# Scores by token halves, paired gate and value weights, and a new issue order in a fused attention and gated MLP kernel

## The chip, the core and the metric

The kernel runs on one core of a Trainium2 chip. A core has five engines with an instruction queue each: TensorE (matrix products, "PE" in the profile, its weight loads "PEld"), VectorE ("DVE"), ScalarE ("ACT"), GpSimd ("POOL") and SyncE ("SP", which here only issues transfers). TensorE writes to PSUM, and VectorE and ScalarE carry results from there into SBUF. The metric is the device time of one execution in microseconds (us), as the median of several runs. A profiled execution gives a trace in which every instruction has a start, a duration and what it waited for.

## The reference

```python
# attention: x is (8, 8, 512, 64), state is (8, 8, 32, 64)
scores  = x @ state^T / sqrt(D);     a  = softmax over the 32 state rows
xread   = a @ state
scores2 = state @ x^T / sqrt(D);     a2 = softmax over the 512 tokens
sread   = a2 @ x
y = concat([xread, sread], axis=2)   # 8 batches, 8 heads, 512 + 32 rows, 64
# gated MLP on y as (8 * 544, 512)
gate = sigmoid(y @ w_gate);  val = y @ w_val      # d_ff = 1536
out  = (gate * val) @ w_out
```

Inputs and output are float32; the kernel computes its products in bfloat16.

## The kernel before

**Algebra.** For the 512 token rows of a batch the product `xread @ w` is never formed from `xread`. The kernel multiplies the state of all heads with the gate and value weights first (`SW`, 8 heads of 32 rows by 1536 columns for each of the two weights), and then multiplies the softmax probabilities with `SW`. So one batch needs: scores, exponentials, sums and products for the probabilities `ab`; their transposes `aT`; `SW`; 12 groups `gv_mm` (four matmuls with 512 columns: two for the gate, two for the value); tanh of the gate half (`gv_th`, ScalarE); the product `glu` (`gv_glu`, VectorE); and 12 groups `out_mm` (four matmuls with `w_out`). The 32 state rows of each batch are read by `rd_mm` and `rd_fin` into `xr`, gathered in `XS`, and go through the MLP together at the end, as "batch 8".

**Tiles.** Tokens are taken as `(p c)`: 128 partitions times four chunks `c`. Head `h` is `2 * j + e` with four pairs `j`. `xT` holds x transposed, in `[j, c]` blocks of 128 by 128; `E1` holds the exponentials in float32 and `Eb` the same in bfloat16. The scores of one batch are 16 matmuls with 64 columns, each with a block of `xT` as its weights; they come in two halves `i` of two head pairs each (`S_mm(b, i, ...)`, `S_exp(b, i)`, `n_sum`, `n_mul`), so each half needs all four chunks of its two pairs.

**Two ways to transpose.** For batches 0 and 1 x and `ab` are transposed on TensorE (`xT_mm`, `aT_mm`) and copied out of PSUM. From batch 2 on, SyncE issues transposing transfers, four for x (`at_xT_dma`, one for each chunk, line 140) and four for `ab` (`aT_dma`, line 211), and one for `xr` (`rd_dma`).

**SW.** `sw_visit(b, lo, n, ...)` computes some columns of `SW` for one batch, `sw_wide(b, v)` half of all columns in three places of PSUM. Each set is eight small matmuls of 64 rows by 32 columns of weights, which lie side by side in the array. Visits of 256 columns do the gate and the value weights one after the other (`sw_mm` twice). `sw_cp` copies one PSUM tile into `SW`, on ScalarE (`act`) or VectorE (`vec`).

**Token sums.** For batches 0 to 2, `rd_mm` gets the sums of `a2` from matmuls with a column of ones, 32 for a batch, each for one head and chunk. From batch 3 on the ones stand beside the x values.

**Weights and loads.** `load_w(w, lo, n)` loads and converts columns of the gate (`w` 0) or value weights (1) through GpSimd's queue, `load_wo` a third of `w_out`, `load_sb` the states of two batches, `load_xh` x of batch 1. SyncE loads x of batch 0 in four pieces of two heads (`load_xp`); batches 2 and 3 come through GpSimd's queue, later ones through SyncE's.

**Order.** The schedule is manual: every engine executes its instructions in the order in which the program text issues them. Lines 415 to 662 are a long list for batches 0 and 1 and the start of batch 2, in which the work of several steps is interleaved by hand. `warm` issues matmuls whose results nobody uses. The loop from line 664 on then has one turn for each batch `b` from 2 to 8, with 12 steps `f`: a `gv_mm` of batch `b` and an `out_mm` of batch `b - 1` in each step, and between them the preparation of batch `nb = b + 1`: `sw_wide` at steps 0 and 6, scores at 1 and 2, sums at 2 and 3, the two products at 4 and 6, `rd_mm` at 6, the four `aT_dma` transposes after step 6, then (for batch 3 as `nb`) the cast and the transposes of the x of the next batch. PSUM has eight places: two for `GV`, one each for `OU` and `AT`, four for `SWP`.

Of the kernel before, what the change touches and what calls it, by code (L numbers as in the profile page):

```python
# [16 lines left out]
def kernel(  # L17
# [42 lines left out]
    wg = wp.tile((128, 4, dff), BF, name="wg")  # L60
    wv = wp.tile((128, 4, dff), BF, name="wv")
# [62 lines left out]
    held = {}  # L124
# [17 lines left out]
    def S_mm(b, i, place, jjs=(0, 1)):  # L142
        if jjs[0] == 0:
            held["S", b, i] = place[0].tile((128, 4, 2, 2, Ns), FP, name="Sp", tag=place[1])
        ps = held["S", b, i]
        for jj in jjs:
            j = 2 * i + jj
            for c in range(4):
                if b < 2:
                    e, c2 = c // 2, c % 2 * 2  # L150
                    nc.tensor.matmul(ps[:, c2:c2 + 2, e, jj], xTs[b][:, j, c], sTd[:, b, 2 * j + e], start=True, stop=True)  # L151
                else:
                    nc.tensor.matmul(ps[:, c, :, jj], xTs[b][:, j, c], sTz[:, b, j], start=True, stop=True)  # L153

    def S_exp(b, i):
        if b not in E1s:
            E1s[b] = ap_.tile((128, 4, 2, 4, Ns), FP, name="E1")
        nc.scalar.activation(E1s[b][:, :, :, 2 * i:2 * i + 2].rearrange("p c e j n -> p (c e) j n"),  # L158
                             held["S", b, i].rearrange("p c e j n -> p (c e) j n"), AF.Exp, scale=scale)

    def at_Eb(b):
        Ebs[b] = ap_.tile((128, 4, 2, 4, Ns), BF, name="Eb")
# [3 lines left out]
    def halfE(b, i):  # L166
        return E1s[b][:, :, :, 2 * i:2 * i + 2].rearrange("p c e j n -> p (c e) j n")

    def n_sum(b, i):
        rs = ap_.tile((128, 8, 2), FP, name="rs")  # L170
        nc.vector.tensor_reduce(rs, halfE(b, i), AX.X, ALU.add)  # L171
        ri = held["ri", b, i] = ap_.tile((128, 8, 2), FP, name="ri")
        nc.vector.reciprocal(ri, rs)

    def n_sums(b):
        rs = ap_.tile((128, 32), FP, name="rs2")
        nc.vector.tensor_reduce(rs, E1s[b].rearrange("p c e j n -> p (c e j) n"), AX.X, ALU.add)
# [3 lines left out]
    def n_muls(b, eng):  # L181
        abs_[b] = ap_.tile((128, 4, 2, 128), BF, name="ab")
        (nc.gpsimd if eng is pool else nc.vector).tensor_tensor(abs_[b].rearrange("p c e (j n) -> p (c e j) n", n=Ns), E1s[b].rearrange("p c e j n -> p (c e j) n"),
                          held["ri", b].unsqueeze(2).to_broadcast((128, 32, Ns)), ALU.mult)

    def n_mul(b, i, eng, lo=0, n=4):
        if b not in abs_:
            abs_[b] = ap_.tile((128, 4, 2, 128), BF, name="ab")
        ri, ce = held["ri", b, i], slice(2 * lo, 2 * lo + 2 * n)
        (nc.gpsimd if eng is pool else nc.vector).tensor_tensor(abs_[b].rearrange("p c e (j n) -> p (c e) j n", n=Ns)[:, ce, 2 * i:2 * i + 2],  # L190
# [559 lines left out]
```

## Time and profile before

| | |
|---|---|
| median of 3 runs | 225.36 us (224.76 to 225.91) |
| the profiled execution | 226.11 us |
| its span in the trace | 224.3 us |
| moved by DMA | 27.13 MB, mean 121 GB/s |
| TensorE's granted clock | 1.00 in every stretch |

The span runs from the first to the last event of the trace; 1.8 us of the profiled execution lie around it. "Busy" is the time in which an engine executes. In a line of the groups or of the timeline, `out<-in` names the tiles written and read, `128*128` or `64*32` behind a matmul is the part of the array that its weights fill, `x8` is the number of instructions, and the bracket at the end names the idle time before and what ended it. For TensorE the durations overlap, since matmuls are pipelined and their ends are modelled; the distance between two starts is what a matmul costs.

### The profile page before, as it was taken

To read this page: it belongs to the slowest core of one execution; us is meant where nothing else is said; L and a number is where in the kernel's file an instruction comes from. 1 tells how busy PE (TensorE), PEld (TensorE's weight loads), DVE (VectorE), ACT (ScalarE), POOL (GpSimd) and SP (SyncE) were. 2 spreads that over 40 slices of the span, in tenths; PEclk is the share of its full clock that TensorE was granted. 3 is DMA by queue.
4 is the path that set the end of the run, shared out by engine and by line. 5 is a ranking of instruction groups with operands and counts; after the bars stand their busy time and mean duration, and the time that the engine had idled before them with its cause. 6 is when DMAs were issued, how large, how long until landed. Compare 5 with 4: busy or idle time off the path is not lost.

```text
span 224.3 us, 5054 instructions
## 1 busy us (share of the span) xinstructions
PE 216.3 (96%) x2001; PEld 106.6 (48%) x2001; DVE 117.3 (52%) x204; ACT 128.6 (57%) x241; POOL 56.3 (25%) x92
## 2 busy tenths in 40 slices
PE   8788999999899999999999999999999999999994
PEld 2554444444344444444444444444444444466744
DVE  2597886476558443843583538544755334422311
ACT  4577785485566566748565666566756444423311
POOL 8299053361323027000720072003200000000001
PEclk9999999999999999999999999999999999999999
DMA  6999999842697233994653203521122111121113
GB/s 192 198 206 190 270 215 173 185 138 44 123 268 265 46 76 88 271 177 123 193 133 92 92 21 73 152 67 47 47 73 76 47 51 47 64 75 50 47 28 114
DMA packets 41911, 27.13 MB, mean 121 GB/s; under 512 B 24000, under 2 KB 38080, under 8 KB 41888
## 3 DMA queue, kind: packets, MB, share of 16 engines
q1 hardware_dynamic: 32544, 18.95, 32.8%
q0 software_dynamic: 9056, 7.67, 19.8%
q8 instruction: 15, 0.25, 0.5%
q10 hardware_dynamic: 288, 0.20, 0.3%
q14 instruction: 8, 0.07, 0.1%
HBM read 18.35 MB, written 8.91 MB: 122 GB/s over the span
## 4 chain that ended last, share of the span: by engine, by line
PE 84%; SPq 6%; DMA 5%; ACT 1%; issue 1%; DVE 1%
PE outp L333 34%; PE gvp L302 34%; PE swp L250 5%; PE gvp L305 5%; SPq L140 4%; DMA xT<-xb 2%; DMA xf<-in_x_dram 2%; SPq L211 2%; PE Sp L153 1%; PE outp L355 1%; PE rdp L225 1%; PE Sp L151 1%; SPq L83 1%; PE warm L369 1%; PE aTp L197 1%
## 5 line engine op out<-in xcount | busy, mean ns | idle before, releaser
L317 DVE SCALAR_TENSOR_TENSOR glu<-th,gvp 128x512 bf16<-128x512 f32 (+1 forms) x108 | 70.5, 658 | 83.9 <-ACT th L312 70.3
L333 PE MATMUL outp<-wo,glu 128*128 128x512 bf16 x396 | 98.2, 379 | 0.0
L302 PE MATMUL gvp<-aT,SW 128*128 128x512 bf16 x384 | 96.3, 379 | 0.1
L312 ACT ACTIVATE th<-gvp 128x512 f32<-128x512 f32 (+1 forms) x108 | 61.8, 576 | 57.5 <-PE gvp L302 44.5
L333 PEld LDWEIGHTS <-glu 128*128 128x128 bf16 x396 | 37.7, 98 | 42.2 <-issue 0.6
L302 PEld LDWEIGHTS <-SW 128*128 128x128 bf16 x384 | 36.2, 98 | 45.0 <-issue 2.8
L288 ACT CAST SW<-swp 128x512 bf16<-128x512 f32 x73 | 40.6, 586 | 7.6 <-PE swp L250 6.9
L337 ACT ACTIVATE res<-outp 128x512 f32<-128x512 f32 x33 | 19.7, 597 | 17.3 <-PE outp L333 17.3
L104 POOL COPY pre<-th 128x1 f32<-128x1 f32 x5 | 0.9, 188 | 69.6 <-ACT th L312 69.6
L116 POOL CAST xb<-xf 128x1024 bf16<-128x1024 f32 x12 | 12.3, 1042 | 15.9 <-DMA xf<-in_x_dram 15.9
L288 DVE CAST SW<-swp 128x512 bf16<-128x512 f32 x23 | 15.4, 684 | 1.3 <-PE swp L250 1.3
L346 POOL DMA_DIRECT2D out_dram<-res x2 | 1.0, 528 | 59.7 <-ACT res L337 59.7
L164 POOL CAST Eb<-E 128x256 bf16<-128x256 f32 x32 | 12.5, 433 | 10.5 <-ACT E L158 10.4
L158 ACT ACTIVATE E<-Sp 128x512 f32<-128x512 f32 x16 | 9.5, 601 | 3.9 <-PE Sp L151 2.4
L214 POOL CAST xs<-xf 128x1024 bf16<-128x1024 f32 x10 | 10.2, 1045 | 0.0
L250 PE MATMUL swp<-wg,sTc 64*32 64x512 bf16 (+1 forms) x192 | 8.7, 327 | 0.0
L190 DVE TENSOR_TENSOR ab<-E,ri 128x512 bf16<-128x512 f32 x11 | 8.5, 771 | 0.0
L171 DVE TENSOR_REDUCE rs<-E 128x16 f32<-128x512 f32 x12 | 8.1, 676 | 0.7 <-ACT E L158 0.7
L369 PE MATMUL warm<-wm 128*128 128x512 bf16 x17 | 6.6, 523 | 1.0 <-DVE wm L417 1.0
L250 PE MATMUL swp<-wv,sTc 64*32 64x512 bf16 (+1 forms) x192 | 7.5, 323 | 0.0
L250 PEld LDWEIGHTS <-sTc 64*32 64x32 bf16 x384 | 4.9, 91 | 5.4 <-issue 3.2
L305 PE MATMUL gvp<-XS,wv 128*128 128x256 bf16 x48 | 7.2, 273 | 0.0
(68 smaller groups left out, 109.3 us busy)
## 6 DMA issues: line engine op xcount, KB each, us to landing
out_dram<-res SPq DMA_DIRECT2D x24, 256.0 KB, 2.6
xf<-in_x_dram SPq DMA_DIRECT2D x4, 1024.0 KB, 7.2
xf<-in_x_dram POOLq DMA_DIRECT2D x2, 1024.0 KB, 8.1
out_dram<-res SPq DMA_DIRECT2D x15, 128.0 KB, 1.9
wo<-in_moe_w_out_dram POOLq DMA_DIRECT2D x3, 512.0 KB, 11.4
xf<-in_x_dram SPq DMA_DIRECT2D x4, 256.0 KB, 3.8
wg<-in_moe_w_gate_dram POOLq DMA_DIRECT2D x2, 512.0 KB, 8.6
wv<-in_moe_w_val_dram POOLq DMA_DIRECT2D x2, 512.0 KB, 10.9
```

The source lines that it names most:

```text
L116: cp(xbs[b].rearrange("p c h d -> p h c d")[:, lo:lo + n], (xhs if b in xhs else xfs)[b][:, lo:lo + n])
L158: nc.scalar.activation(E1s[b][:, :, :, 2 * i:2 * i + 2].rearrange("p c e j n -> p (c e) j n"), held["S", b, i].rearrange("p c e j n -> p ( ...
L164: nc.gpsimd.tensor_copy(Ebs[b][:, c], E1s[b][:, c])
L214: pool(xs.rearrange("p c h d -> p h c d")[:, lo:lo + n, :, :D], xfs[b][:, lo:lo + n])
L250: nc.tensor.matmul(pss[e][j * Ns:(j + 1) * Ns, o:o + n], sTc[rows, b, j] if b > 1 else sTd[rows, b, 2 * j + e, e], (wg, wv)[w][rows, j, lo ...
L288: cp(*sw_left.pop((b, lo, w, e)))
L302: nc.tensor.matmul(ps, SWs[b][:, g, w, fs], aTs[b][:, :, g], start=(g == 0), stop=(g == 1))
L305: nc.tensor.matmul(ps, (wg, wv)[w][:, j, fs], XS[:, :, j], start=(j == 0), stop=(j == 3))
L312: nc.scalar.activation(th, held["gv", b, f][0], AF.Tanh, scale=0.5)
L317: nc.vector.scalar_tensor_tensor(glus[b][:, f], held["th", b, f], 1.0, held["gv", b, f][1], ALU.add, ALU.mult)
L333: nc.tensor.matmul(ops[b, c], glus[b][:, f, c * 128:(c + 1) * 128], wo[:, f], start=(f == 0), stop=(f == NF - 1))
L337: nc.scalar.activation(res, ops[b, c], AF.Copy, scale=0.5)
```

## The change

Six parts. (1) From batch 2 on, a half of the scores is two chunks of tokens with all four head pairs, not two head pairs with all chunks; `E1`, `Eb`, sums and products follow (`half`, `grp`), and `aT_dma(b, i)` sends two of the four transposes. In the loop the first two go out at step 5 and the other two at step 6. (2) Gate and value weights lie in one tile `wgv`. (3) `sw_pair` computes 256 gate and 256 value columns with one matmul of 512 columns, in place of two `sw_mm`. (4) The token sums of batches 0 to 2 take all four head pairs in one matmul, 8 for a batch. (5) The hand-written list is new throughout: loads, casts, copies, the places in PSUM and the order of the groups. The matmul groups in it are the same, and so is the number of `warm` matmuls, 17. (6) Some work moves to other engines in that list: the second part of batch 2's x is still cast on GpSimd but the first on VectorE, half of batch 3's on ScalarE.

The helpers:

```diff
-    wg = wp.tile((128, 4, dff), BF, name="wg")
-    wv = wp.tile((128, 4, dff), BF, name="wv")
+    wgv = wp.tile((128, 4, 2, dff), BF, name="wgv")
+    wg, wv = wgv[:, :, 0], wgv[:, :, 1]
...
     def S_mm(b, i, place, jjs=(0, 1)):
+        if b > 1:
+            ps = held["S", b, i] = place[0].tile((128, 2, 2, 4, Ns), FP, name="Sp", tag=place[1])
+            for c in range(2):
+                for j in range(4):
+                    nc.tensor.matmul(ps[:, c, :, j], xTs[b][:, j, 2 * i + c], sTz[:, b, j], start=True, stop=True)
+            return
...
+    def half(b, i, t):
+        if b > 1:
+            return t[b][:, 2 * i:2 * i + 2].rearrange("p c e (j n) -> p (c e j) n", n=Ns)
+        return t[b].rearrange("p c e (j n) -> p (c e) j n", n=Ns)[:, :, 2 * i:2 * i + 2]
...
-    def aT_dma(b):
-        for c in range(4):
+    def aT_dma(b, i):
+        for c in range(2 * i, 2 * i + 2):
             nc.sync.dma_start_transpose(aT_tile(b)[:, c], abs_[b][:, c].rearrange("p e k -> p (e k)"))
...
-            if b < 3:
-                for c in range(4):
-                    for j in range(4):
-                        nc.tensor.matmul(rd[j * Ns:(j + 1) * Ns, e, D:], Ebs[b][:, c, e, j], ones, start=(c == 0), stop=(c == 3))
+        for e in range(2 if b < 3 else 0):
+            for c in range(4):
+                nc.tensor.matmul(rd[:, e, D:], Ebs[b][:, c, e], ones, start=(c == 0), stop=(c == 3))
...
+    def sw_pair(pss, b, lo, n):
+        for j in range(4):
+            for e in range(2):
+                rows = slice(e * 64, (e + 1) * 64)
+                nc.tensor.matmul(pss[e][j * Ns:(j + 1) * Ns].rearrange("p (w n) -> p w n", w=2),
+                                 sTc[rows, b, j] if b > 1 else sTd[rows, b, 2 * j + e, e],
+                                 wgv[rows, j, :, lo:lo + n], start=True, stop=True)
...
-            for w in range(2):
-                sw_mm(pss, b, w, lo, n, w * n)
+            sw_pair(pss, b, lo, n)
...
-                for w in range(2):
-                    sw_mm(pss, b, w, lo + 512, 256, 256 * w)
+                sw_pair(pss, b, lo + 512, 256)
```

The loop:

```diff
+                if f in (5, 6):
+                    aT_dma(nb, f - 5)
                 if f == 6:
-                    aT_dma(nb)
                     rd_dma(nb)
```

The start of the new list, which takes the place of lines 415 to 473 and on:

```python
load_xp(0, nc.sync, 6, 2)
nc.vector.memset(wm, 0.0)
warm(1, GV)
warm(2, GV)
warm(4, SWP)
zero(sTz, pool)
load_xp(0, nc.sync, 0, 2)
load_s(0, nc.scalar)
zero(sTd, vec)
make_identity(nc, ident)
load_xh(1, 0, 4)
load_xh(1, 4, 4)
cast_xp(0, vec, 0, 2)
cast_s(0, act)
warm(1, GV)
sT_mm(0, SWP)
cast_xp(0, act, 6, 2)
sT_pad(0, act)
xT_mm(0, 3, OU)
load_xp(0, nc.sync, 4, 2)
sT_pad(1, vec)
load_w(1, 256, 256)
cast_xp(0, pool, 4, 2)
xT_mm(0, 0, GV)
xT_cp(0, 0, act)
xT_mm(0, 2, SWP)
warm(1, SWP)
xT_cp(0, 3, vec)
load_w(0, 256, 256)
xT_cp(0, 2, vec)
S_mm(0, 1, GV, (0,))
load_xp(0, nc.sync, 2, 2)
S_mm(0, 0, SWP, (0,))
cast_xp(0, act, 2, 2)
xT_mm(0, 1, OU)
zero(sbz, vec)
xT_cp(0, 1, vec)
S_mm(0, 1, SWP, (1,))
...
S_exp(0, 1)
n_sum(0, 1)
...
load_w(0, 1024, 512)
...
S_exp(0, 0)
...
n_sum(0, 0)
n_mul(0, 0, vec)
load_w(1, 1024, 512)
```

Its later places that matter below: the groups of batches 0 and 1 up to the cast of batch 2 on VectorE, and the way from batch 2's scores to the loop.

```python
sw_visit(0, 1024, 512, 1)
sw_cp(0, 1024, 1, 1, vec)
aT_cp(1, None, vec)
sw_cp(0, 1024, 1, 0, act)
sw_visit(1, 1024, 512, 1)
gv_mm(0, 11, GV)
...
load_x(2, nc.gpsimd)
...
sw_cp(0, 0, 2, 0, vec)
cast_x(2, vec, 0, 4)
gv_mm(1, 4, SWP)
gv_th(0, 4)
...
gv_glu(0, 4)
...
cast_x(2, pool, 4, 4)
gv_th(1, 5)
at_xT_dma(2)
...
S_mm(2, 0, GV)
...
S_exp(2, 0)
S_mm(2, 1, OU)
S_exp(2, 1)
n_sum(2, 0)
n_sum(2, 1)
...
n_mul(2, 0, vec)
out_mm(0, 6, GV)
load_x(3, nc.gpsimd)
at_Eb(2)
n_mul(2, 1, pool)
sw_wide(2, 1)
sw_cp(2, 1, 1, 0, act)
aT_dma(2, 0)
...
aT_dma(2, 1)
...
cast_x(3, pool, 4, 4)
cast_x(3, act, 0, 4)
out_mm(0, 7, GV)
sw_wide(2, 0)
at_xT_dma(3)
```

More of the change, by code (lines that the diff above doesn't have):

```diff
@@ L522 @@
[L522 to L532 removed]
+    gv_mm(0, 11, GV)
+    sw_cp(1, 1024, 1, 0, act)
+    gv_th(0, 11)
+    gv_mm(0, 8, SWP)
+    gv_glu(0, 11)
+    gv_mm(0, 10, GV)
+    gv_th(0, 8)
+    gv_th(0, 10)
+    sw_cp(1, 1024, 1, 1, vec)
+    load_w(1, 0, 256)
+    gv_glu(0, 8)
+    sT_mm(2, AT)
+    sw_visit(1, 512, 512, 1)
@@ L664 @@
+    sw_cp(2, 0, 1, 1, vec)
     for b in range(2, B + 1):
```

449 lines of the change are left out of this document (205 added, 244 removed).

## The prediction

> **What bounds the kernel now.** I read the shares of the engines first, then the chain that ended last, then the span by stages.
>
> ```profile
> span 224.3 us, 5054 instructions
> PE 216.3 (96%) x2001; PEld 106.6 (48%) x2001; DVE 117.3 (52%) x204; ACT 128.6 (57%) x241; POOL 56.3 (25%) x92
> ```
>
> ```profile
> PE 84%; SPq 6%; DMA 5%; ACT 1%; issue 1%; DVE 1%
> ```
>
> TensorE (PE) is busy 96% and is 84% of the chain; the rest of the chain is mostly SyncE's queue (SPq) and transfers. In the stages below, the columns are the stretch, its length and each engine's busy time, then clock, DMA share and GB/s. I cut them where the matmuls of batch 0 begin to follow without a break (20.91), and at the first gate matmul of batches 2, 3, 4 and 5.
>
> ```profile
> 0.00:20.91 20.91, 17.08 (x306) 9.15 (x306) 12.59 (x26) 12.23 (x22) 15.70 (x31) 1.00 1.17 198
> 20.91:57.10 36.19, 36.19 (x408) 16.50 (x401) 26.19 (x44) 24.75 (x47) 13.61 (x17) 1.00 0.90 169
> 57.10:81.50 24.40, 23.49 (x216) 10.86 (x208) 13.33 (x23) 15.16 (x29) 5.60 (x9) 1.00 0.63 164
> 81.50:105.34 23.84, 23.50 (x216) 10.83 (x208) 12.73 (x23) 15.13 (x29) 5.57 (x9) 1.00 0.67 148
> 105.34:128.67 23.33, 23.33 (x216) 10.83 (x209) 12.73 (x23) 14.99 (x29) 5.57 (x9) 1.00 0.48 135
> ```
>
> From 20.91 on TensorE has no gaps except in the turns of batches 2 and 3. They last 24.40 and 23.84 us, the next one 23.33, with 216 matmuls in each: 1.07 + 0.51 = 1.58 us are waiting, and its cause stands in TensorE's waits (total, times, longest).
>
> ```profile
> PE Sp L153 <- DMA xT<-xb: 1.3, 2, 0.9
> ...
> PE swp L250 <- issue: 0.8, 1, 0.8
> ```
>
> So there are three places where time can go: the start before 20.91, the solid stretch 20.91 to 57.10, which only fewer or cheaper matmuls or a new stall can alter, and the 1.58 us. After 105.34 only cheaper matmuls could gain.
>
> **Matmuls that become fewer.** The changed program issues 1802 matmuls instead of 2001: 128 fewer in the gate and value weights (256 of 256 columns become 128 of 512), 72 fewer for token sums. What these cost now (start, length, instruction group; I use the distance from start to start, because the ends are modelled):
>
> ```profile
> 80.95 0.40 PE L250 MATMUL swp<-wv,sTc 64*32 64x512 bf16 x8
> 81.17 0.29 PE L250 MATMUL swp<-wg,sTc 64*32 64x256 bf16 x8
> 81.28 0.29 PE L250 MATMUL swp<-wv,sTc 64*32 64x256 bf16 x8
> 81.50 1.04 PE L302 MATMUL gvp<-aT,SW 128*128 128x512 bf16 x4
> ```
>
> Eight matmuls of 512 columns take 0.22 us, eight of 256 take 0.11. The time goes by columns and not by instructions: a pair of 0.11 + 0.11 becomes one of 0.22. I cost the edit at nothing, and the steady turn stays 23.33.
>
> ```profile
> 52.82 0.25 PE L232 MATMUL rdp<-ones,Eb 128*32 128x1 bf16 x16
> 52.92 0.33 PE L228 MATMUL rdp<-xb,Eb 128*32 128x64 bf16 x16
> 53.06 0.30 PE L232 MATMUL rdp<-ones,Eb 128*32 128x1 bf16 x16
> 53.28 0.30 PE L250 MATMUL swp<-wg,sTd 64*32 64x256 bf16 x8
> ```
>
> ```profile
> 87.44 0.40 PE L153 MATMUL Sp<-sTz,xT 128*128 128x64 bf16 x8
> 87.68 1.03 PE L333 MATMUL outp<-wo,glu 128*128 128x512 bf16 x4
> 88.54 0.81 PE L302 MATMUL gvp<-aT,SW 128*128 128x512 bf16 x3
> ```
>
> The 32 token sums of a batch take 0.10 + 0.22 = 0.32 us, four at a time side by side with 32 columns of weights. Eight take their place, each with all 128 columns of weights; the nearest row is the score matmul of that form, 0.24 us for eight. That is a gain of 0.08 for each of three batches at best and, if the wider loads hide worse, a loss of about as much: nothing, within 0.3 us in all. A big matmul costs (88.54 - 87.68) / 4 = 0.215 us.
>
> The same group of eight lasts 0.11 us where its own form follows (81.17 to 81.28) and 0.22 where another does (81.28 to 81.50). A rule of the Trainium skill speaks of this and against the edit: TensorEngine Tiling (Array Packing), Key Properties, says that a change of tiling mode drains TensorE. The trace agrees, with 0.11 us. By the rule the wide sums add one such change where weight matmuls follow them, in batch 1: the sum below would be 0.1 higher.
>
> **The start.** The new order loads heads 6, 0, 4, 2 of batch 0 (before 4, 2, 6, 0) and puts casts and copies on other engines.
>
> ```profile
> 9.54 1.26 ACT L158 ACTIVATE E<-Sp 128x512 f32<-128x512 f32 x2 [1.55 <-PE Sp L151]
> ```
>
> ```profile
> 7.48 0.43 DVE L91 CAST xf<-xf 128x512 bf16<-128x512 f32 x1 [1.16 <-DMA xf<-in_x_dram]
> ...
> 20.86 0.68 DVE L288 CAST SW<-swp 128x512 bf16<-128x512 f32 x1
> ```
>
> The last load of batch 0 lands at 7.48 and 2.06 us later the first exponential starts. After the change only its cast (0.43 by the row; ScalarE does it), four transposes and four score matmuls stand between, without the copies of the other heads that stood there: I estimate 8.7, 0.8 earlier. VectorE's sums then start at 9.35 instead of 10.17, where the first stretch below begins. From there VectorE is the narrow place: the last copy that the first group of eight after the start needs (20.86) ended at 21.54.
>
> ```profile
> 10.17:21.54 11.37, 9.65 (x18) 1.00 1.37 199
> 21.54:30.50 8.96, 8.08 (x16) 1.00 1.27 252
> ```
>
> ```profile
> L190 DVE TENSOR_TENSOR ab<-E,ri 128x512 bf16<-128x512 f32 x11 | 8.5, 771 | 0.0
> ```
>
> The first two lines are VectorE's busy times in two stretches. In the first it had 9.65 busy and 1.72 idle. The change swaps one copy for another of 0.68 and brings one product from GpSimd (0.77 by the third line), so 10.4 us. From 9.35 the copy ends at 19.8 with no idle left and at 21.5 with all of it; TensorE begins 0.63 before that, as now (21.54 - 20.91): 19.1 to 20.9.
>
> The second condition is a load. The value weights of columns 1024 on were issued at 6.03:
>
> ```profile
> 6.03 0.79 POOL L100 DMA_DIRECT2D wv<-in_moe_w_val_dram  x1
> ...
> 20.53 0.93 POOL L78 DMA_DIRECT2D xf<-in_x_dram  x1
> ...
> 30.50 1.04 POOL L116 CAST xb<-xf 128x1024 bf16<-128x1024 f32 x1 [7.55 <-DMA xf<-in_x_dram]
> ```
>
> ```profile
> DMA to landing us min/median/max: 5.9/7.9/13.0
> ```
>
> ```profile
> L111 POOL MEMSET sTz<- 128x2048 bf16 x1 | 1.8, 1822 | 0.0
> ```
>
> The landing line is for all eight weight loads, so they landed by 19.0 at the latest. In the new order GpSimd first clears a tile twice as large as now (1.82 us, so 0.9 more) and casts two heads between the issues (about 0.5, half of the cast at 30.50): with a short wait for these heads I put the issue at 7.6. The DMA share is 1.17 over the whole start, the engines are full, and the same bytes stand ahead of this load, so its landing should move less than its issue: 19.0 to 20.6. Its matmuls and a copy (0.22 and 0.68 us, less the 0.63 lead) put TensorE's start some 0.5 later with the hand-overs, 19.5 to 21.1. I take 20.2 from both, **0.7 us gained**. Whether the 0.8 us of "issue" comes back I cannot see; I count it neither way.
>
> **The solid stretch.** It holds the same 34 groups of four big matmuls, the same copies and transposes, so it keeps its 36.19 us unless a new wait comes in.
>
> ```profile
> L91 DVE CAST xf<-xf 128x512 bf16<-128x512 f32 x3 | 1.6, 538 | 4.5 <-DMA xf<-in_x_dram 4.5
> ```
>
> The change adds three waits. ScalarE casts half of batch 3, whose load is issued about when it was and well ahead; behind the cast stand copies of weight products out of PSUM, for which TensorE's next weight matmuls wait. SyncE's first half of the probability transposes waits for the first product only; behind it stand the second half, the x transposes of batch 3 and output stores. VectorE casts half of batch 2 (before GpSimd). In 21.54 to 30.50 VectorE is busy 8.08 of 8.96; two casts of 0.54 by the row above, or a little more, make 9.2 to 9.4, over by 0.2 to 0.4. Behind the cast stand the products (glu) of the gates; three pairs of PSUM buffers cover some of it. I take **0.3 us lost**, bounds 0 and 0.9.
>
> **Scores by token halves.** The first half of the scores now needs two of the four x transposes, and two of the four probability transposes leave one step earlier.
>
> ```profile
> 53.98 5.84 SPq L140 DMA_TRANSPOSE xT<-xb  x4
> ```
>
> ```profile
> 58.55 3.12 DMA xT<-xb
> ```
>
> Batch 3's four go out from 53.98 to 59.82, the last is issued at 58.55 and lands at 61.67, and the longest wait of the scores for it is the 0.9 above: they wanted it at 60.8. Two of them would have landed at about 53.98 + 1.46 + 3.12 = 58.6. The second half, two big groups (1.72 us) later, can wait until 62.5. Batch 4's queue starts earlier as well, for half of batch 3's probabilities no longer stand in it after the turn's middle. I take 1.4 of the 1.58 us, **1.4 gained**, bounds 0.5 and 1.58. Batches 5 to 7 show no such wait, and gain nothing.
>
> **Sum.** -0.7 + 0.3 + 0 - 1.4 = -1.8. The profiled execution took 226.11, so 224.3. That execution lies 0.75 above the median of 225.36; on the level of the medians it is **223.6 us**.
>
> **Rivals.**
> 1. *The loads bind the start.* DMA share 1.17 to 1.37 says that the start is full, and a new order cannot bring all weights earlier. Then TensorE starts at 20.9 as now and with 0.3 lost only 1.1 remains: 225.0, or 224.3 on the medians' level. The Trainium skill (DMA: Bandwidth & Descriptors, Issuing engines are not separate DMA queues) says that transfers of all issuers share 16 engines; this case's share above 1 agrees.
> 2. *The halves do nothing.* If the x transposes of batch 3 go out as late as now plus a stall, or the halves wait for all four landings, the 1.58 us stay: 226.11 - 0.4 = 225.7, 225.0 on that level. Against it: the landings are waited for one by one.
> 3. *VectorE waits for batch 2's x: slower.* That load was issued at 20.53 and GpSimd's cast found it landed at 30.50, 10.0 us later; only GpSimd waited for it. In the new order TensorE, from 20.2, does nine big groups (7.7), six weight visits (1.3) and three small ones of state transposes (0.24 each, as scores) before the groups that stand behind VectorE's cast: it is at 30.0. Three groups (2.6) and the first half of a fourth (0.4) go on without VectorE, to 33.0; the cast (1.1) and one product (0.7) must be done by then, so a landing until 31.2 is free. Later, each us costs one, and from 33.3 the gains of 2.1 are gone. The issue moves to 19.1 to 20.9 (five issues behind batch 1's casts, or the landing above), so 29 to 31 is likely; with the longest weight latency, 13.0, it is 33.9. At 36 the time is 226.11 - 2.1 + 4.8 = 228.8, 228.1 on that level.
>
> **Chances.** Forecast 0.53; a better start (19.2, and no loss after it) at 222.3, 0.07; rival 1 0.12; rival 2 0.11; rival 3, or another new wait as dear, 0.17. About 0.5% (1.1 us) is what a measurement of this kernel can tell from no change. Faster 0.62 (the forecast without its worst 0.04, the better start and half of rival 1), same 0.21 (those 0.04, the other half and rival 2), slower 0.17. All bounds at their best (start 19.1, no loss, 1.58, sums 0.2) make 221.8; all at their worst (start 21.1, loss 0.9, sums 0.3, halves 0.5) 226.3. I give 221.8 to 226.6, which leaves most of rival 3 out.
>
> **What would show it.** Right: the first exponential near 8.7, the unbroken gate matmuls from about 20.2, turns of batches 2 and 3 near 23.4 with no score waiting for a transpose, eight paired weight matmuls in 0.22. Wrong: VectorE idle before its cast of batch 2, score waits as before, a weight wait at 19 to 21 that lasts over 1 us, or new idle time of TensorE between 21 and 57.

## The result and the profile after

The changed kernel takes **223.81 us** (median of 10 runs, 223.13 to 224.29); the kernel before took 225.24 us beside it (10 runs). The ratio is 0.994, with an interval of 0.9913 to 0.9967: faster by 0.6%. Here and below the ratios leave disturbed runs out, so one can differ a little from the quotient of the medians. The profiled execution took 223.65 us, 2.46 less than the one of before (226.11), so the two traces differ by 1.0 us more than the medians do.

The page of after, its span, its engines' busy times and its chain of what ended last:

```profile
span 221.9 us, 4663 instructions
PE 214.9 (97%) x1801; PEld 103.8 (47%) x1801; DVE 118.3 (53%) x209; ACT 129.0 (58%) x241; POOL 53.8 (24%) x90
...
PE 89%; DMA 7%; SPq 2%; issue 0%; ACT 0%; POOL 0%; DVE 0%
```

The span by stages of after, cut at the same events as before (start of the unbroken gate matmuls, first gate matmul of batches 2, 3 and 4), with the same columns:

```profile
0.00:19.10 19.10, 15.77 (x241) 8.08 (x241) 13.01 (x26) 12.62 (x21) 15.82 (x30) 1.00 1.13 197
19.10:55.33 36.23, 36.23 (x344) 15.92 (x337) 27.42 (x48) 24.88 (x48) 10.43 (x16) 1.00 0.99 178
55.33:79.58 24.25, 23.49 (x200) 10.61 (x192) 12.61 (x22) 15.15 (x29) 6.12 (x9) 1.00 0.86 176
79.58:102.91 23.33, 23.33 (x201) 10.57 (x193) 12.74 (x23) 15.00 (x29) 5.57 (x9) 1.00 0.71 149
```

The stretches were 20.91, 36.19, 24.40 and 23.84. So the start gave 1.81 us, the solid stretch lost 0.04, and the turns of batches 2 and 3 gave 0.15 and 0.51: 2.43 in all, which is the difference of the spans. The sum came out about as forecast, but not its terms: the start gave more than twice the 0.7, and the halves less than half of the 1.4.

TensorE's waits in after that touch the change (total, times, longest); a wait for "issue" is no longer among them:

```profile
PE Sp L147 <- DMA xT<-xb: 0.8, 1, 0.8
...
PE swp L266 <- DMA wgv<-in_moe_w_gate_dram: 0.2, 1, 0.2
```

Two things are therefore to be explained: why the issue wait of 0.8 us is gone, and why a score wait of nearly the old length is still there. The timeline of TensorE in after shows the second one, and the timeline of SyncE's queue shows what it waits for:

```profile
58.79 0.40 PE L147 MATMUL Sp<-sTz,xT 128*128 128x64 bf16 x8
...
60.75 0.28 PE L147 MATMUL Sp<-sTz,xT 128*128 128x64 bf16 x4
61.80 0.29 PE L147 MATMUL Sp<-sTz,xT 128*128 128x64 bf16 x4 [0.76 <-DMA xT<-xb]
```

```profile
47.46 6.00 SPq L221 DMA_TRANSPOSE aT<-ab  x4
53.56 5.13 SPq L140 DMA_TRANSPOSE xT<-xb  x4
```

The first half of batch 3's scores finds its two transposes there; the second half waits 0.76 us for the last one. SyncE sends these transposes at 53.56, only 0.42 earlier than before (53.98), while TensorE has come 1.81 earlier out of the start. The chain of what ended last shows when the last of the four was issued and how long it took to land:

```profile
57.43 4.32 DMA xT<-xb
```

It was issued 1.12 earlier than before (58.55) but took 4.32 us to land instead of 3.12, so it landed at 61.75, as late as before (61.67). The first three of these four took 2.4 to 2.5; with that the last would have been there at 59.9, ahead of TensorE.

### The profile page after: what moved, and what is told of

Its sections match the earlier page's. It is cut to its first block, busy times and chain, and to the rows that moved or that the text cites. A ratio compares the mean times of both kernels' runs of the same rounds, so it can differ in the third digit from the quotient of the medians.

```text
span 221.9 us, 4663 instructions
## 1 busy us (share of the span) xinstructions
PE 214.9 (97%) x1801; PEld 103.8 (47%) x1801; DVE 118.3 (53%) x209; ACT 129.0 (58%) x241; POOL 53.8 (24%) x90
## 3 DMA queue, kind: packets, MB, share of 16 engines
q1 hardware_dynamic: 32544, 18.95, 36.3%
## 4 chain that ended last, share of the span: by engine, by line
PE 89%; DMA 7%; SPq 2%; issue 0%; ACT 0%; POOL 0%; DVE 0%
PE gvp L317 37%; PE outp L348 37%; PE gvp L320 5%; PE swp L259 4%; DMA wgv<-in_moe_w_gate_dram 3%; DMA xT<-xb 2%; DMA xf<-in_x_dram 2%; SPq L140 2%; PE swp L266 2%; PE outp L370 1%; PE Sp L147 1%; PE rdp L235 1%; SPq L83 0%; PE stp L410 0%; PE rdp L238 0%
## 5 line engine op out<-in xcount | busy, mean ns | idle before, releaser
L327 ACT ACTIVATE th<-gvp 128x512 f32<-128x512 f32 (+1 forms) x108 | 61.7, 574 | 59.9 <-PE gvp L317 47.6
L303 ACT CAST SW<-swp 128x512 bf16<-128x512 f32 x70 | 39.2, 584 | 6.3 <-PE swp L259 4.7
L303 DVE CAST SW<-swp 128x512 bf16<-128x512 f32 x26 | 17.3, 684 | 1.1 <-PE swp L266 0.8
L173 POOL CAST Eb<-E 128x256 bf16<-128x256 f32 x32 | 11.8, 402 | 12.0 <-ACT E L167 12.0
L116 POOL CAST xb<-xf 128x1024 bf16<-128x1024 f32 x10 | 10.6, 1087 | 11.2 <-DMA xf<-in_x_dram 7.3
L320 PE MATMUL gvp<-XS,wgv 128*128 128x256 bf16 x96 | 11.9, 273 | 0.0
L320 PEld LDWEIGHTS <-wgv 128*128 128x128 bf16 x96 | 9.4, 98 | 3.0
L181 DVE TENSOR_REDUCE rs<-E 128x16 f32<-128x512 f32 x14 | 9.4, 673 | 1.2 <-ACT E L167 1.2
L200 DVE TENSOR_TENSOR ab<-E,ri 128x512 bf16<-128x512 f32 x13 | 9.1, 709 | 0.0
L259 PE MATMUL swp<-wgv,sTc 64*32 64x512 bf16 x192 | 7.6, 381 | 0.0
L147 PEld LDWEIGHTS <-xT 128*128 128x128 bf16 x96 | 4.4, 98 | 3.5 <-DMA xT<-xb 0.9
```

Of the source, the lines that this page charges most:

```text
L116: cp(xbs[b].rearrange("p c h d -> p h c d")[:, lo:lo + n], (xhs if b in xhs else xfs)[b][:, lo:lo + n])
L173: nc.gpsimd.tensor_copy(Ebs[b][:, c], E1s[b][:, c])
L259: nc.tensor.matmul(pss[e][j * Ns:(j + 1) * Ns, o:o + n], sTc[rows, b, j] if b > 1 else sTd[rows, b, 2 * j + e, e], (wg, wv)[w][rows, j, lo ...
L303: cp(*sw_left.pop((b, lo, w, e)))
L320: nc.tensor.matmul(ps, (wg, wv)[w][:, j, fs], XS[:, :, j], start=(j == 0), stop=(j == 3))
L327: nc.scalar.activation(th, held["gv", b, f][0], AF.Tanh, scale=0.5)
```

## The experiments

Twelve runs were made, each beside the kernel before. The results, with what the one trace of each shows of the start and of the loop (all in us, and waits as the profile lists them):

| run | median us | ratio to before (interval) | unbroken gate matmuls from | issue wait in the start | waits for x transposes (total) |
|---|---|---|---|---|---|
| before, first trace | 225.24 | | 20.91 | 0.82 | 1.3 |
| before, second trace | 225.34 | 0.9994 (0.9963 to 1.0026) | 20.89 | 0.38 | 0.8 |
| after | 223.81 | 0.994 (0.9913 to 0.9967) | 19.10 | none | 0.8 |
| halves only | 224.69 | 0.9974 (0.9957 to 0.9991) | 20.39 | 0.61 | none |
| pairs and sums only | 224.27 | 0.9968 (0.9942 to 0.9993) | 19.08 | none | 1.2 |
| list only | 226.19 | 1.0047 (1.0022 to 1.0072) | 21.65 | 1.55 | 1.7 |
| list and halves | 224.79 | 0.9984 (0.9957 to 1.0012) | 20.06 | 1.32 | 0.8 |
| all but the list | 223.88 | 0.9932 (0.9901 to 0.9962) | 19.14 | none | none |
| after, halves undone | 224.67 | 0.9977 (0.9956 to 0.9999) | 19.50 | none | 1.2 |
| before, 64 small matmuls | 226.88 | 1.0066 (1.0035 to 1.0097) | 21.80 | 0.85 | 0.9 |
| before, 25 small matmuls | 227.57 | 1.003 (0.9992 to 1.0069) | 18.95 | none | 4.3 |
| after, fillers swapped | 223.48 | 0.9929 (0.9903 to 0.9956) | 19.93 | 1.13 | none |
| after, second half later | 222.43 | 0.989 (0.9855 to 0.9924) | 18.58 | none | none |
| after, GpSimd's clear late | 226.74 | 1.0047 (1.0014 to 1.008) | 23.00 | none | 1.1 |

### One part alone

**Halves only.** The kernel before with the scores and the softmax of batches 2 to 7 by token halves:

```diff
+        if b > 1:
+            ps = held["S", b, i] = place[0].tile((128, 2, 2, 4, Ns), FP, name="Sp", tag=place[1])
+            for c in range(2):
+                for j in range(4):
+                    nc.tensor.matmul(ps[:, c, :, j], xTs[b][:, j, 2 * i + c], sTz[:, b, j], start=True, stop=True)
+            return
...
+                if f in (5, 6):
+                    aT_dma(nb, f - 5)
                 if f == 6:
-                    aT_dma(nb)
                     rd_dma(nb)
```

> The kernel before with the token halves alone (scores, exponentials, products and probability transposes of batches 2 to 7 by chunks; old list, old weight tiles, old token sums). Theory that the halves remove the waits of the loop wherever the x transposes leave: in the old list they leave at the same times as before, so the scores of batches 3 and 4 find their first two transposes landed; the turns of batches 2 and 3 fall from 24.40 and 23.84 to 23.4 each, and the time falls by 1.1 to 1.5 us; the start up to 20.9 stays. Rival, that the halves gain next to nothing and the list did all: the turns stay above 24.2 and 23.8, time within 0.3 us of before.

No score matmul of the loop is listed as waiting for a transpose here, though the last four of batch 3 still start 0.33 us later than the pace of the others, with their transpose landing at 63.03. The turns of batches 2 and 3 last 23.64 and 23.32, 1.28 less than in the first trace of before and near the 1.4 of the prediction. The start is still that of before, with the issue wait; its trace around it:

```profile
17.82 0.42 PE L260 MATMUL swp<-wg,sTd 64*32 64x512 bf16 x5
18.85 0.39 PE L260 MATMUL swp<-wg,sTd 64*32 64x512 bf16 x3 [0.61 <-issue]
```

A group of eight weight matmuls is cut after its fifth. Its last three start 1.03 us after its first, and neither a semaphore nor a transfer stands behind the wait. With 0.26% (0.6 us) the halves alone are worth less than that in the time, also because a new wait of 0.62 us for a copy comes ahead of the loop.

**Pairs and sums only.** The kernel before with `wgv` in one tile, `sw_pair` for two calls of `sw_mm`, and eight wide token sums for 32 narrow ones:

```diff
+            sw_pair(pss, b, lo, n)
-            for w in range(2):
-                sw_mm(pss, b, w, lo, n, w * n)
...
+        for e in range(2 if b < 3 else 0):
+            for c in range(4):
+                nc.tensor.matmul(rd[:, e, D:], Ebs[b][:, c, e], ones, start=(c == 0), stop=(c == 3))
```

> The kernel before with the paired gate and value weights and the 8 token sums alone. Theory that TensorE's time goes by columns: nothing changes, turns 23.33 as before, time within 0.3 us. Rival, that the 0.8 us in which TensorE stood under issue at 18.5 hangs on the number of instructions ahead of it: the stall moves or goes with 200 matmuls fewer, the unbroken gate matmuls begin at 20.1 instead of 20.9, and the time falls by up to 0.8 us.

The part that the prediction had costed at nothing starts the gate matmuls at 19.08, as early as the whole change, and gives 0.32% (0.7 us), with the old order of loads. The score waits of the loop stay (0.77 and 0.48).

**List only.** The kernel after with the halves, the pairs and the sums undone.

> The changed kernel with halves, pairs and the 8 token sums all undone, so the old helpers in the new list; both halves of the probability transposes leave after step 6 again. Theory that the list alone makes the start: unbroken gate matmuls begin at 19.1 to 19.3 as in the changed kernel, first exponential at 8.3, and the first scores of batches 3 and 4 wait for x transposes again, so turns near 24.4 and 23.8; time 1.2 to 1.8 us below before. Rival, that the fewer instructions made part of the start: the issue stall of 0.8 us is back and the gate matmuls begin near 19.9.

Slower than before. The issue wait is twice as long and stands at another place of the program; the timeline of TensorE and then the stretches 15 to 20 and 20 to 25 of this run:

```profile
15.26 0.22 PE L239 MATMUL rdp<-ones,Eb 128*32 128x1 bf16 x10
17.02 0.21 PE L239 MATMUL rdp<-ones,Eb 128*32 128x1 bf16 x6 [1.55 <-issue]
```

```profile
15.00:20.00 5.00, 3.45 (x87) 1.35 (x87) 2.48 (x4) 2.57 (x6) 4.29 (x7) 0.80 1.45 193
20.00:25.00 5.00, 5.00 (x53) 2.35 (x52) 4.48 (x8) 3.32 (x6) 2.15 (x3) 0.85 1.41 199
```

The granted clock (the third number from the end) is 0.80 and 0.85 around and after the pause, and was 1.00 in the stretches of before. From the end of the wait to the unbroken gate matmuls it took 4.63 us here and 3.30 in the run "list and halves" below, whose clock stayed at 1.00; so some 1.3 us of the 21.65 go with the lower clock. In ten of the twelve executions of this kernel the mean clock was 0.998 or higher, so its start is likely earlier in those than in this trace. The trace holds other waits too: 1.7 us of score waits in the loop, and 0.5 of a gate group for probability transposes.

**What the three have in common.** Counted from the first matmul on, the wait comes after matmul 222 in before and in halves only, and after 223 in list only: the same count at three different places of the work. That speaks for the supply of instructions and not for a wait of the work itself. The profile shows the supply as a queue of its own, here in the transfer view of before in the 0.1 us from 16.90 and of after from 14.60:

```profile
q8 instruction: 1, 0.02, 59.1%
```

```profile
q8 instruction: 1, 0.02, 59.3%
```

One packet of 0.02 MB each. The page of before counts 15 such packets with 0.25 MB, about 16 KiB a packet; that of after, with 200 matmuls fewer, counts 14. Against the ends of the issue waits, with the distance from the middle of the 0.1 us in which the packet stands:

```
run                      packet at   wait ends   distance   wait after matmul
before                   16.9        19.36       2.4        222
before, second trace     17.0        19.35       2.3        222
halves only              16.4        18.85       2.4        222
list only                14.7        17.02       2.3        223
list and halves          14.3        16.76       2.4        223
```

So the wait ends 2.3 to 2.4 us after a packet of instructions. In after the packet comes at 14.6, its instructions would be there at 17.0, and matmul 222 (the fifth of the eight transposes at 17.89) is reached at 18.1: no wait. The Trainium skill (Runtime: NRT & Kernel Launch, Instruction fetch mechanics) says that instructions are fetched in blocks of 16 KiB, 256 instructions, by a queue of the sequencer's own, and that the cost of a block's boundary is mostly hidden. The trace agrees on the size and on the queue; here the boundary cost up to 1.55 us.

### The count of instructions by itself

**64 and 25 small matmuls in before.** Matmuls of one column, whose results nobody reads, in place of two and of one of the ten warm-up matmuls, while TensorE waits for the first data:

```diff
-    warm(2, GV)
+    small(64, 0, GV)
```

```diff
-    warm(2, GV)
+    small(25, 1, GV)
```

> Kernel before, with 64 matmuls of one column in place of two of the ten warm-up matmuls, before any data has landed, where TensorE only waits; all else as before. Theory A (TensorE's instructions come in blocks: the next block is asked for when about the 111th matmul passes and is there 5.2 us later; the stall falls after the 222nd matmul if that one comes sooner): the 111th matmul is now in the group of score matmuls at 9.9, the block is there at 15.1, and the 222nd matmul is one of the token sums at 14.9. The 0.82 us of issue at 18.5 go, at most 0.3 comes at about 15, the unbroken gate matmuls start at 20.1 to 20.3 and the time falls by 0.5 to 0.8 us (224.4 to 224.7 against 225.2), with 62 matmuls more. Theory B (the 0.8 us belong to the place: something that the weight matmuls at 18.5 wait for and that the profile does not name): the stall of 0.8 stays at 18.5 and the time is 225.2 or a little more.

> Kernel before, with 25 matmuls of one column in place of one of the ten warm-up matmuls, in the same place as in the run with 64. Theory A (supply in blocks): the 111th matmul is now one of the transposes at 13.4, the next block is there at 18.6, and the 222nd matmul is in the first gate group, at 16.1: a stall of about 2.4 us there, instead of 0.82 at 18.5. The unbroken gate matmuls start at about 21.8 (before 20.91) and the time rises by about 0.9 us, to 226.1, more if the clock falls after the pause. Theory B (the stall belongs to the place): 0.8 at 18.5 as before, 225.2. Theory C (more instructions always cost): the loss grows with the number of added matmuls, so this run lies between before and the run with 64.

Both expectations had a spacing of 111 matmuls between two blocks and were wrong in it; the traces gave the spacing. With 64 small matmuls there was no wait after matmul 222, but one after 350:

```profile
20.01 0.29 PE L232 MATMUL rdp<-ones,Eb 128*32 128x1 bf16 x15
21.15 0.16 PE L232 MATMUL rdp<-ones,Eb 128*32 128x1 bf16 x1 [0.85 <-issue]
```

350 is 222 + 128, and a matmul is two instructions, its weight load and itself: 256 instructions, one block. Its packet came at 18.8, again 2.3 us ahead of the end of the wait. With 25 small matmuls no boundary is met too early: the packet for the boundary after 222 came at 12.4, and the unbroken gate matmuls began at 18.95, with 24 matmuls more and nothing changed in the work: 2.0 us earlier than before, 0.8 of it because the first scores ran at 8.11 instead of 8.88. So the wait follows the count and not the place, and more instructions can cost nothing. The times of these two don't bear the comparison out: both took warm-up matmuls away, the mean clock was 0.992 or lower in seven of the twelve executions with 64, and with 25 the scores of batch 2 waited 3.3 us for transposes in the profiled execution. I read only the waits and the starts, and of the run with 64, whose granted clock was 0.86 and 0.80 in the stretches 5 to 10 and 10 to 15, the wait alone.

**Fillers swapped in after.** The same, without touching the warm-up and with the spacing known:

```diff
-    warm(2, OU)
+    small(32, 1, OU)
```

> Kernel after, with one of the two warm-up matmuls at 14.01 (512 columns, 0.215 us) replaced by 32 matmuls of one column (0.007 us each where such were seen, so also about 0.22): the same filling time, 31 matmuls more between the two boundaries, no work of the kernel touched. Theory A, as mended by the run with 64 (instructions come in blocks of 256, that is 128 matmuls; the boundary lies after the 222nd matmul, and the block is usable 2.4 us after its 16 KiB packet, which came at 14.6 in after): the 222nd matmul is now a token sum at 15.9, the block is there at 17.0: an issue stall of about 1.0 us at 15.9 to 17.0, unbroken gate matmuls from 20.0 to 20.3 instead of 19.10, time 0.8 to 1.1 over after (224.6 to 224.9, or more if the clock falls). Theory B (the stall in before came from its narrow matmuls or their waits and not from the count): as after, 223.8.

The wait came where it was expected, after matmul 222 and with 1.13 us for the expected 1.0, and ended 2.4 us after the packet at 14.3. The timeline of TensorE in this run, there and at batch 3's scores:

```profile
15.44 0.20 PE L241 MATMUL rdp<-ones,Eb 128*128 128x1 bf16 x2
16.77 0.29 PE L241 MATMUL rdp<-ones,Eb 128*128 128x1 bf16 x6 [1.13 <-issue]
...
19.93 1.42 PE L317 MATMUL gvp<-aT,SW 128*128 128x512 bf16 x5
...
61.57 0.40 PE L147 MATMUL Sp<-sTz,xT 128*128 128x64 bf16 x8
```

But the time did not rise: 223.48, as after. The gate matmuls began 0.83 later, and the 0.76 of score wait was gone. That is not only because TensorE came later to the second half of batch 3's scores (61.57). The last x transpose landed at 60.46 here and at 61.75 in after, so it would have been there even for the TensorE of after, which was ready for it at 61.0. The queue of the instructions tells the two traces apart once more. With 31 matmuls more ahead, a block is fetched at an earlier place of the program: here a packet stands at 57.12, before the last transpose was issued (57.53), and in after at 59.30, between its issue (57.43) and its landing. The transfer view of after in the 0.1 us from 59.30:

```profile
q8 instruction: 1, 0.02, 59.9%
```

This holds across the runs. Of the 53 x transposes of batch 3 whose landing the fourteen traces give, nine took 3.9 to 4.6 us, and each of the nine has an instruction packet of 16 KiB between its issue and its landing; the other 44 took 2.4 to 3.2, two of them with a packet in the first 0.5 us of their flight. That the packet holds the transfer up is likely from this and not shown, since no run moved the packet alone: this one moved the start too.

**List and halves.** The kernel after with the pairs and the sums undone: the count of before, with the rest of the change.

> Kernel after with the paired weights undone (two matmuls of 256 columns for one of 512) and the 32 narrow token sums back: the new list and the halves without the fewer matmuls. Theory A (supply in blocks): the issue stall is back near 15.4, at about 1.5 us as in the run of the list alone, the unbroken gate matmuls start at 20.6 to 21.7, turns of batches 2 and 3 are 23.4 to 23.7; 225.0 to 225.6, so 1.2 to 1.8 over after. The prediction's own step (fewer matmuls are worth nothing, the list gives the start its gain): as after, 223.8, within 0.3.

The issue wait is back (1.32 us, at 16.76), the gate matmuls begin at 20.06 and the time is 224.79, a little below what was expected. Without the fewer matmuls the change gains 0.16%, which can't be told from nothing.

### The list, the halves and the wait that is left

**All but the list.** The kernel before with halves, pairs and sums, in its own order of loads.

> Kernel before with its own order of loads and head work, but with the scores and softmax by token halves, the paired weights and the eight wide token sums: the whole change but the list. Theory A (the start's gain comes from the fewer matmuls, which end the stall, and not from the list): no issue stall, unbroken gate matmuls from about 19.1 as in after, turns of batches 2 and 3 together no more than 0.8 over two steady turns of 23.33: 223.6 to 224.0 as after, or below if the later part of the head keeps its cover. Theory B (the list has its own share of the start, as the prediction had it with 0.7): unbroken gate matmuls from 19.8 or later and 224.3 or more.

0.9932 against 0.994 of the whole change: the new list adds nothing that these runs show. The gate matmuls begin at 19.14. This kernel has no reserve: its packet comes at 16.0, so the block is there at 18.4, and matmul 222 is the fifth of eight token sums that begin at 18.25. Pairs and sums only is as close: its packet comes at 15.9, and matmul 222 starts at 18.16 and the next at 18.38.

**Halves undone in after.**

> Kernel after with the token halves undone: scores and softmax of batches 2 to 7 by head halves as in before, all four probability transposes issued together in the later step. Paired weights, token sums and list stay. The prediction's step (halves gain 1.4 of 1.58 us): turns of batches 2 and 3 together 46.66 + 1.58 plus what the earlier start adds, because the x transposes of batch 3 leave only 0.4 us earlier while TensorE comes 1.8 earlier: 1.6 to 3.0 us of score waits, 224.6 to 225.9. Rival 2 (the halves do nothing, the waits are as in after): 223.8.

```profile
59.17 0.50 PE L153 MATMUL Sp<-sTz,xT 128*128 128x64 bf16 x3
60.84 0.32 PE L153 MATMUL Sp<-sTz,xT 128*128 128x64 bf16 x5 [1.17 <-DMA xT<-xb]
```

This is the timeline of TensorE. The first half of the scores, which needs all four transposes again, waits 1.17 us, and batch 2's turn, from the gate matmul at 55.71 to the next batch's at 80.62, is 24.91 instead of 24.25. The turns of batches 2 and 3 hold 1.58 over two steady ones, just under the 1.6 to 3.0 expected. The time is 0.9 above after; in the traces 0.66 of the difference is the turn and 0.40 a later start, which had waited 0.68 for gate weights and is no work of the halves.

**Second half of batch 3's scores one step later.**

```diff
-                if f in (1, 2):
-                    S_mm(nb, f - 1, AT)
-                    S_exp(nb, f - 1)
+                if f in ((1, 3) if nb == 3 else (1, 2)):
+                    S_mm(nb, f // 2 if nb == 3 else f - 1, AT)
+                    S_exp(nb, f // 2 if nb == 3 else f - 1)
```

> Kernel after with the second half of batch 3's scores (and its exponential) one step of the loop later, 1.72 us. Theory A (the 0.76 us that are left are the wait for the last x transposes of batch 3, which land at 61.8): the wait goes, the turn of batch 2 falls from 24.25 to 23.4 to 23.6, nothing new waits, 223.0 to 223.3. Theory B (another stage takes the time up, as the exponential and the products of batch 3 come later): the probability transposes of batch 3 are late, a gate group waits in the turn of batch 3, and the time is 223.8 or more.

The stretches of this run, cut as before:

```profile
0.00:18.58 18.58, 16.63 (x241) 8.53 (x242) 13.04 (x26) 12.63 (x21) 16.05 (x30) 1.00 1.16 202
18.58:54.81 36.23, 36.10 (x342) 15.94 (x337) 27.34 (x48) 24.94 (x48) 10.16 (x16) 1.00 0.99 179
54.81:78.16 23.35, 23.19 (x197) 10.55 (x193) 12.50 (x22) 15.06 (x29) 6.08 (x9) 1.00 0.92 183
```

The turn of batch 2 is 23.35, no wait is left in the loop, and none came in its place, although the last x transpose took 4.37 us here too. With 222.43 us, 1.1% below before, this is the fastest of all, and below the 223.0 to 223.3 expected. The gain over after, 1.4 us between the medians and 1.1 by the ratios (whose intervals touch), is more than the 0.76. In the traces it is 0.90 in the turn of batch 2 and 0.52 in the start, since this execution began its gate matmuls at 18.58, and without the wait an early start counts in full.

**GpSimd's clear late.** The kernel after with the clear of `sTz` behind the loads of the last weights instead of ahead of batch 1's x:

```diff
-    zero(sTz, pool)
...
     load_wo(2)
+    zero(sTz, pool)
```

> The changed kernel with the clearing of the 1.8 us tile moved on GpSimd behind the loads of the output weights, so that x of batch 1 and the weights are issued 1.8 us earlier. Theory that the later issue of batch 1's x let batch 0's x land sooner: now the last piece of batch 0 lands near 7.4 again instead of by 6.7, the first exponential moves from 8.3 to about 9, and the unbroken gate matmuls begin 0.3 to 0.8 later than 19.1. Rival, that the issue of the weights binds the start: the first weight matmuls, which waited 0.2 us for their load at 13.45, start up to 0.3 earlier and the gate matmuls begin at 18.7.

The clear, which the prediction saw only as a delay, does the start good. Without it batch 1's x and the first weights are issued 1.54 us earlier, and the last heads of batch 0 come late, although their own issue has not moved. First GpSimd's timeline of after and the time that the four loads of batch 0's x took to land in it, then the same two of this run, then this run's timeline of TensorE and its stretches 5 to 10 and 10 to 15:

```profile
3.00 1.70 POOL L96 DMA_DIRECT2D xf<-in_x_dram  x2
```

```profile
DMA to landing us min/median/max: 3.6/4.0/4.4
```

```profile
1.46 1.71 POOL L96 DMA_DIRECT2D xf<-in_x_dram  x2
```

```profile
DMA to landing us min/median/max: 3.6/4.0/7.0
```

```profile
9.94 0.61 PE L132 MATMUL xTp<-ident,xf 128*128 128x128 bf16 x4 [2.05 <-ACT xf L91]
```

```profile
5.00:10.00 5.00, 1.88 (x26) 1.09 (x23) 2.75 (x5) 1.78 (x3) 2.79 (x4) 0.83 1.36 212
10.00:15.00 5.00, 5.00 (x34) 3.21 (x35) 3.65 (x8) 2.21 (x3) 2.84 (x6) 0.50 1.31 204
```

In after these transposes run at 7.76, so they are 2.18 later here, after a wait of 2.05 us. The granted clock then is 0.83 and 0.50, where after has 1.00, and the rest of the way to the gate matmuls takes 1.72 longer. That goes with this kernel and not with the one trace: in ten of its twelve executions the mean clock was 0.992 or lower. The gate matmuls begin at 23.00, 3.9 later, where 0.3 to 0.8 was expected: the direction was right and the size was not. The time is 0.5% over before. The prediction's picture that the same bytes stand ahead, so that landings move less than issues, does not hold for batch 0's x.

**Before again.** No edit.

> Kernel before, unchanged, for a second trace of it: whether the start at 20.91, the issue stall of 0.82 us and the score waits of 0.9 and 0.5 us in the first trace are its own or of that one execution. If they are its own: stall 0.6 to 0.9 after the 222nd matmul, 2.4 us after a packet of instructions; unbroken gate matmuls 20.3 to 20.9, moved by the landing of the last heads of batch 0 alone; score waits 1.0 to 1.6 together; time 225.0 to 225.3.

The start at 20.9 is before's own, its parts are not: here the first scores run at 9.31 (8.88 in the first trace) and the issue wait is 0.38. The score waits are not either: the turns of batches 2 and 3 hold 1.00 over two steady ones (24.33 and 23.32) and not the 1.58 from which the prediction took its 1.4. Where the data of batch 0 come later, matmul 222 is reached later and finds less to wait for.

## Why the prediction was right, and where it was not

**The time.** 223.6 was forecast and 223.81 came. The sum held because two terms were wrong in opposite directions; that it came within 0.2 us is luck.

**The start, -0.7 expected, -1.81 in the traces.** The term was mis-sized, and the step of it that failed is the one about fewer matmuls, "I cost the edit at nothing". By the time of the matmuls it was right (its 1802 matmuls are 1801: 2001 less 128 and 72, as the page of after has it). TensorE's timeline of after, first the weight matmuls of a visit and then the token sums:

```profile
47.07 0.63 PE L259 MATMUL swp<-wgv,sTc 64*32 64x512 bf16 x16
47.51 0.40 PE L266 MATMUL swp<-wgv,sTc 64*32 64x512 bf16 x8
...
48.19 0.35 PE L241 MATMUL rdp<-ones,Eb 128*128 128x1 bf16 x8
48.41 0.81 PE L348 MATMUL outp<-wo,glu 128*128 128x512 bf16 x3
```

Sixteen matmuls of 512 columns take 0.44, as 0.22 for eight says, and eight wide sums take 0.22, even 0.10 less than the 32 narrow ones. What the step did not see is that instructions, too, have a supply: fewer of them ahead of a boundary means that TensorE comes to it later in time. That took the 0.8 us of "issue" away, which the prediction counted neither way. From the first score matmuls to the unbroken gate matmuls it was 12.03, 11.58 and 11.81 us in the three traces of the old list with the issue wait (before twice, halves only) and 10.99, 10.85 and 10.84 in those without (pairs and sums only, all but the list, 25 small matmuls): 0.9 shorter on average, in the last case with more matmuls instead of fewer.

The other part of the 1.81 is no gain of the change as far as these runs show. The first scores ran at 8.09 to 9.31 in seven traces of the old list; they depend on when batch 0's last heads land, and before's first trace (8.88) was one of the late ones. It agrees with this that the traces differ by 2.46 and the medians by 1.43.

**The list.** The first exponential came at 8.30 (8.7 expected, 9.54 before), so the step-by-step reading of the new order was about right, and it didn't matter: the start that the list was to bring forward is 19.14 without it and 18.58 to 19.50 with it in the three traces that have no issue wait (the run with the late clear apart). Alone the list is 0.5% slower than before: it brings matmul 222 to 15.3, where its block is not there until 17.0, and the score waits of the loop stay. With the halves added (list and halves, with a wait of 1.32) the time can't be told from before.

**The solid stretch, +0.3 expected, +0.04 came.** VectorE's cast of batch 2 stands at 31.28 without a wait, just behind the 31.2 up to which I had put a landing as free, and no gate group behind it was late. The over-full stretch of VectorE, from which the 0.3 came, was worked out too tightly. Rival 3 did not happen.

**The halves, -1.4 expected, -0.66 came.** The mechanism was right: alone they bring the turns of batches 2 and 3 to within 0.3 of steady ones, and undone they lengthen batch 2's turn by 0.66. The size was off in after, by two steps. The prediction set the landing against when TensorE wanted the scores in the trace of before (60.8, and 62.5 for the second half), though its own first term had moved TensorE forward: TensorE came to the second half at 61.0. And it took for the last transpose the 3.12 us from issue to landing of before, where 4.32 came; with 3.12 it would have landed at 60.55, and nothing would have waited. So score waits nearly as before, one of the prediction's own signs of being wrong, stood in the trace of after. The fewer matmuls seem to have a part in both: they moved TensorE forward, and they put an instruction packet (59.30) into the flight of the last transpose. The run with the later second half shows what comes back when the wait is out of the way.

**The rivals.** Rival 1 (loads bind the start) holds in small: waits of 0.2 and 0.7 for gate weights stand in two traces, but the gate matmuls began well ahead of 20.9. Rival 2 is out with the run of the halves alone. What stays open is why the packet of instructions comes 1.0 to 3.6 us after the boundary ahead of it (matmul 94, by the spacing of 128) was passed, and whether it is the instruction packet that makes an x transpose land late: no run separated these.

## What to carry to other kernels

A short stall of "issue" that stands at the same count of instructions in every version is the supply of instructions: count the matmuls ahead of it, fillers and narrow ones included, and ask whether a dense stretch of small ones reaches the boundary too early. When a transfer lands late in one version and not in another, look whether a packet of instructions lies between its issue and its landing. When two edits gain one after the other in time, work the second one out on the timeline that the first one leaves. A start that has become faster is worth only what the next transfer on its way lets through, so look for that wait and move the step that meets it.

## What the hardware showed unexpectedly

- TensorE stopped for 0.38 to 1.55 us at matmul 222 or 223, once at 350, and went on 2.3 to 2.4 us after a packet of the instruction queue (about 16 KiB), in seven traces. Replacing one filler matmul of 512 columns by 32 of one column was enough to bring 1.13 us of it.
- In the profiled execution with the longest of these pauses, 1.55 us, the granted clock was 0.80 and 0.85 in the two stretches of 5 us around and after it; after pauses of 1.32 and 1.13 us in two other runs it was 1.00. In the run with the late clear it was 0.83 and 0.50 around and after a wait of 2.05 us. No run separated pause and clock.
- Nine x transposes of batch 3 took 3.9 to 4.6 us to land, each with a 16 KiB instruction packet between issue and landing; the 44 others took 2.4 to 3.2.
- With batch 1's x and the first weights issued 1.54 us earlier on GpSimd, a load of batch 0's x that SyncE had issued at the same time as before took 7.0 us to land instead of at most 4.4, and TensorE's work on the last heads came 2.2 us later.
